# Seven PSUM areas of their own, and two instructions for a three-bank exponential

## The chip, the cores and the metric

The kernel runs on one core of a Trainium2 chip. The metric is the device time of one execution in microseconds, lower being better. A run's profile is one execution recorded by the hardware profiler; its span goes from the first to the last instruction. PE is the matrix engine (PEld its weight loads), ACT the scalar engine, DVE the vector engine, POOL a third elementwise engine, SP the queue that issues most DMAs.

## The reference

One input `x` of 2048 rows by 640 columns goes through a layer norm. Attention with 32 heads of 20 columns reads it, and so does a gated layer with 1728 hidden columns. The attention output is multiplied by a silu of the gated layer, and `x` is added:

```python
xn = _layernorm(x)
qkv = (xn @ wqkv).reshape(B, S, 3, 32, 20).transpose(2, 0, 3, 1, 4)
p = softmax(einsum("bhqd,bhkd->bhqk", q, k) * 20 ** -0.5)
s = einsum("bhqk,bhkd->bhqd", p, v).transpose(0, 2, 1, 3).reshape(B, S, D) @ wo
h = sigmoid(xn @ w_gate) * (xn @ w_up)
out = x + s * silu(h @ w_down)
```

The weights are `wqkv` 640 x 1920, `wo` 640 x 640, `w_gate` and `w_up` 640 x 1728, `w_down` 1728 x 640. Everything is bf16 at the borders.

## The kernel before

**Start.** The rows come in four chunks of 512. DVE makes the statistics, ACT and POOL write the normalised tiles `xn` (two each per chunk, lines 244 and 247), PE transposes them (line 252), ACT and DVE copy the result to `xnT` (lines 256 and 258). The keys of the first group of heads and the first queries follow.

**Attention.** Four heads make a group; there are eight groups and four chunks of 512 queries, so 32 blocks, each with 16 key tiles x 4 heads = 64 score jobs. A job is one score matmul of 32 x 128 by 32 x 512 into one PSUM bank (2 KB per partition; there are eight banks), an exponential, and one value matmul that adds 21 x 512 into a quarter of the accumulator `oacc`, one bank. Score matmuls of up to four heads run side by side on PE, and so do four value matmuls.

The exponential has two ways. On ACT (`exp_act`, line 81) one instruction takes a whole slot of PSUM: `scA3` has three banks, `scA2` two, and they alternate. On DVE it is made of integers: `iv` (line 747) reads one bank, `scD`, and after four heads of a key tile four passes `pb` (line 625) follow over all of them, and the value matmul is done for each pass (so four times, with scaled values `vs`). At most four of the 16 key tiles of a block go this way; `claim_dve` gives them out and `claim_act` the others.

**Side work.** Keys, queries and values of the next blocks, the gated layer (gate and up `mk_gu`, tanh `tnh` on ACT, product `hT` on DVE, then the down projection `mk_down` with `td` and `gqs`, which is parked in DRAM as `gq_dram`) and the output projection (`mk_out`, one piece per 128 rows and half of the columns) all use one bank, `misc`, one after another: a piece has its matmuls, then its ACT and DVE steps, and only then does the bank go to the next.

**Normalisation.** At a block's end DVE copies `oacc` to `on` (line 593). The row sums go through DRAM (`ld`, `lt`), are inverted (`rt`, line 603), go through DRAM again (`rd`, `rl`), POOL multiplies (line 610), and DMAs put the block into `oU` with heads along partitions, as the output projection needs it.

**Order.** The orders of PE, ACT and DVE are fixed while the kernel is built, by a planner that steps a clock (`now`) and has a cost for each instruction (`T_F`, `T_PV`, `T_MM`, a charge `T_MODE` where PE changes between score matmuls, F, value matmuls, PV, and side work, M). Its clock only sets the order; on the chip each engine goes through its list and waits for semaphores. Pieces of the gated layer are tied to blocks 0 to 27 and taken one at a time as `misc` comes free. What is left when the blocks end is written out behind them, piece by piece. The buffers for ACT's exponentials are `pt0` (three of three banks) and `pt1` (four of two):

```python
SLOT = (3, 2)
scA = [psum.tile([P, n, 512], FP32, name=f"scA{n}", tag=f"scA{n}") for n in SLOT]
scD = psum.tile([P, 512], FP32, name="scD", tag="scD")
NPT, NPB, NIV = (3, 4), 2, 2
```

## Time and profile before

| | us |
|---|---|
| median of 3 runs | 966.5 (958.08 to 977.37) |
| the profiled execution | 965.4 |
| its span | 963.7 |
| PE busy | 867.8 (90%) |
| ACT busy | 802.9 (83%) |
| DVE busy | 768.1 (80%) |
| POOL busy | 107.3 (11%) |

Busy time counts an instruction from its start to its end. On ACT, DVE and PE the next one can begin before that end, so the pace of an engine is read from one start to the next, in the timeline. An idle time in brackets is that of the engine before the row, with what ended it. Names such as `scA_428` carry a buffer number: 428 is the slot of three banks, 429 that of two. A view can join rows that follow each other (`x4`).

### The profile page before, as it was taken

What the parts mean: (1) busy time and instruction counts of PE and PEld (TensorE: products, weight loads), DVE (VectorE), ACT (ScalarE), POOL (GpSimd) and SP (SyncE); (2) the same over time, 40 slices, a digit from 0 to 9 for tenths busy, and PEclk for the clock granted to TensorE, in tenths of its full rate; (3) what the DMA queues carried; (4) which work ended last, traced back from release to release, by engine and by line L of the source; (5) the groups of instructions that cost most, each with busy time, mean ns of one, the idle gap of its engine ahead of it and who ended that gap; (6) DMA issues with size and microseconds to landing.
All of it is one profiled execution on the core that took longest, in us unless ns stands there. A gap on an engine that the chain in (4) does not pass through costs nothing.

```text
span 963.7 us, 18399 instructions
## 1 busy us (share of the span) xinstructions
PE 867.8 (90%) x7285; PEld 306.8 (32%) x7372; DVE 768.1 (80%) x1302; ACT 802.9 (83%) x790; POOL 107.3 (11%) x152
## 2 busy tenths in 40 slices
PE   3799999999999999999999999999999999997664
PEld 1333323333333233332333333333233322223332
DVE  6588889898888888888888889898888888883122
ACT  3769998989999898979999999999999899981000
POOL 4110010110001000100000000110000000000044
PEclk9799999999999999999999999999999999998889
DMA  8301211112110211111110111102121111211366
GB/s 215 126 10 43 49 44 33 47 48 53 30 38 29 52 44 41 45 42 46 45 42 20 41 33 44 44 16 64 44 58 30 38 50 45 62 44 31 109 185 184
DMA packets 85798, 54.53 MB, mean 57 GB/s; under 512 B 33552, under 2 KB 79440, under 8 KB 85712
## 3 DMA queue, kind: packets, MB, share of 16 engines
q1 hardware_dynamic: 84560, 52.05, 19.7%
q8 instruction: 57, 0.93, 0.4%
q10 hardware_dynamic: 1152, 1.31, 0.4%
q14 instruction: 29, 0.24, 0.1%
HBM read 42.32 MB, written 8.39 MB: 53 GB/s over the span
## 4 chain that ended last, share of the span: by engine, by line
PE 49%; ACT 24%; DVE 18%; issue 5%; DMA 3%; POOL 1%; SPq 0%; POOLq 0%; DVEq 0%; another core or an unknown queue 0%; ACTq 0%
PE oacc L580 13%; PE mps L402 10%; DVE pb L625 7%; PE scA_428 L540 6%; PE mps L425 5%; DVE iv L747 5%; PE scA_429 L540 5%; PE scD L540 4%; PE mps L457 2%; PE mps L372 2%; PE mps L341 1%; DVE ob L464 1%; PE mps L352 1%; DMA ob<-gq_dram 1%; DVE hT L410 1%
## 5 line engine op out<-in xcount | busy, mean ns | idle before, releaser
L747 DVE TENSOR_SCALAR iv<-scD 128x512 int16<-128x512 f32 x452 | 310.0, 686 | 95.4 <-PE scD L540 85.9
L625 DVE TENSOR_SCALAR pb<-iv 128x2048 int16<-128x2048 int16 x452 | 307.9, 714 | 3.0
L402 PE MATMUL mps<-xnT,wgu 128*128 128x512 bf16 (+1 forms) x505 | 150.9, 385 | 7.7 <-DVE hT L410 1.4
L610 POOL TENSOR_TENSOR on_bf<-on,rl 128x512 bf16<-128x512 f32 x32 | 42.7, 1335 | 558.0 <-DMA rl<-rd 341.6
L540 PE MATMUL scD<-q,kT_69 32*128 32x512 bf16 x228 | 87.9, 385 | 2.3 <-DVE iv L747 1.8
L425 PE MATMUL mps<-wd,hT 128*128 128x320 bf16 x448 | 80.9, 306 | 8.6 <-DVE gqs L435 7.5
L540 PE MATMUL scD<-q,kT_70 32*128 32x512 bf16 x224 | 85.6, 382 | 2.1 <-DVE iv L747 1.8
L580 PE MATMUL oacc<-pb,vs_74 128*21 128x512 bf16 x684 | 80.2, 382 | 1.7 <-DVE pb L625 1.2
L580 PE MATMUL oacc<-pb,vs_73 128*21 128x512 bf16 x672 | 79.7, 382 | 1.6 <-DVE pb L625 1.3
L540 PEld LDWEIGHTS <-kT_70 32*128 32x128 bf16 x1024 | 38.5, 91 | 123.4 <-issue 119.4
L540 PEld LDWEIGHTS <-kT_69 32*128 32x128 bf16 x1024 | 39.2, 91 | 120.8 <-issue 113.9
L402 PEld LDWEIGHTS <-wgu 128*128 128x128 bf16 (+1 forms) x560 | 44.1, 98 | 85.1 <-issue 58.4
L540 PE MATMUL scA_428<-q,kT_69 32*128 32x512 bf16 x478 | 64.5, 387 | 7.4 <-DVE q L168 3.2
L540 PE MATMUL scA_428<-q,kT_70 32*128 32x512 bf16 x480 | 64.8, 383 | 4.6 <-ACT pt_2941 L81 0.5
L540 PE MATMUL scA_429<-q,kT_70 32*128 32x512 bf16 x320 | 64.0, 383 | 1.4 <-ACT pt_3070 L81 0.4
L540 PE MATMUL scA_429<-q,kT_69 32*128 32x512 bf16 x318 | 63.3, 386 | 1.4 <-ACT pt_7252 L81 0.5
L425 PEld LDWEIGHTS <-hT 128*128 128x128 bf16 x448 | 38.9, 98 | 49.4 <-issue 37.4
L457 PE MATMUL mps<-wo,oU 128*128 128x320 bf16 x160 | 31.2, 332 | 23.1 <-DVE ob L464 22.1
L464 DVE SCALAR_TENSOR_TENSOR ob<-mps,ob 128x320 f32<-128x320 f32 x32 | 15.7, 492 | 38.2 <-PE mps L457 31.1
L81 ACT ACTIVATE tnh<-mps 128x512 bf16<-128x512 f32 (+1 forms) x56 | 35.6, 636 | 10.5 <-PE mps L402 10.5
L410 DVE SCALAR_TENSOR_TENSOR hT<-tnh,mps 128x512 bf16<-128x512 bf16 (+1 forms) x56 | 38.1, 681 | 4.4 <-PE mps L402 3.9
L580 PEld LDWEIGHTS <-v_71 128*21 128x21 bf16 x1024 | 27.7, 90 | 41.1 <-issue 33.0
(1374 smaller groups left out, 1754.5 us busy)
## 6 DMA issues: line engine op xcount, KB each, us to landing
rl<-rd SPq DMA_DIRECT2D x128, 64.0 KB
wgu<-in_B_w_gate_dram SPq DMA_DIRECT2D x24, 320.0 KB
wgu<-in_B_w_up_dram SPq DMA_DIRECT2D x24, 320.0 KB
gq_dram<-gqs SPq DMA_DIRECT2D x32, 160.0 KB
ob<-gq_dram SPq DMA_DIRECT2D x16, 320.0 KB
ob<-in_A_x_dram SPq DMA_DIRECT2D x16, 160.0 KB
out_dram<-ob SPq DMA_DIRECT2D x16, 160.0 KB
oU<-on_bf SPq DMA_DIRECT2D x112, 20.0 KB
```

Of the source, the lines that this page charges most:

```text
L81: return nc.scalar.add_instruction(mybir.InstActivation(func=func, name=nc.get_next_instruction_name(), engine=ENG.Activation, ins=[nc.sca ...
L372: nc.tensor.matmul(st["ps"][:, i * 2 * GC:(i + 1) * 2 * GC], lhsT=xnT[:, kd, tts[i] * P:(tts[i] + 1) * P], rhs=wvs[pr][:, kd, :], start=(k ...
L402: nc.tensor.matmul(st[key][0:fs, :], lhsT=w[:, i, kd, ko * P:ko * P + fs], rhs=xnT[:, kd, c * QC:(c + 1) * QC], start=(kd == 0), stop=(kd ...
L410: nc.vector.scalar_tensor_tensor(out=hT[0:fs, kf, :], in0=st["t"][0:fs, :], scalar=1.0, in1=st["u"][0:fs, :], op0=ALU.add, op1=ALU.mult)
L425: nc.tensor.matmul(st["ps"][:, 0:HD], lhsT=hT[0:fsz[kf], kf, t4 * P:(t4 + 1) * P], rhs=wd[0:fsz[kf], kf, h * HD:(h + 1) * HD], start=(kf = ...
L457: nc.tensor.matmul(st["ps"][:, 0:HD], lhsT=oU[:, kd, tt * P:(tt + 1) * P], rhs=wo[:, kd, h * HD:(h + 1) * HD], start=(kd == 0), stop=(kd = ...
L464: nc.vector.scalar_tensor_tensor(out=tmp, in0=st["ps"][:, 0:HD], scalar=0.25, in1=gqr[:, sl], op0=ALU.mult, op1=ALU.mult)
L540: nc.tensor.matmul(dst, lhsT=kTs[(b // NQC) % 2][32 * j:32 * j + 32, kt * P:(kt + 1) * P], rhs=qs[b][32 * j:32 * j + 32, :], start=True, s ...
L580: nc.tensor.matmul(oacc[32 * j:32 * j + DH + 1, :], lhsT=lhsT, rhs=u["src"], start=first, stop=last, tile_position=(0, 32 * j), skip_group ...
L610: nc.gpsimd.tensor_tensor(out=on_bf, in0=on, in1=rl, op=ALU.mult)
L625: nc.vector.tensor_scalar(out=pb[:, k, :, :].bitcast(I16), in0=iv, scalar1=0.25, scalar2=cst, op0=ALU.mult, op1=ALU.add)
L747: nc.vector.tensor_scalar(out=d["iv"][:, j, :], in0=scD, scalar1=I_OFF, scalar2=I_LOW, op0=ALU.add, op1=ALU.max)
```

## The change

The eight banks are divided anew: two slots of two banks (`scA`), three single banks (`bank`), which are tensors of their own, and `oacc`. A fill of a slot has two banks, or three where the single bank with the slot's number (0 or 1) is free. Such a fill is two ACT instructions, one over the single bank and one over the slot. Single banks are also used by the DVE way and by side work: bank 2 first, and banks 0 and 1 for side work only when it is behind a schedule (`due`), which spreads it evenly to a little before the last four blocks. The gated layer is no longer tied to blocks but taken whenever this schedule has room. Several side pieces can be under way, and their later steps wait for events (`pre`, `gates`).

The planner is rewritten with it: other costs, a step of 0.02 instead of 0.04, rules on when PE leaves one kind of matmul for another (`URGENT`, `HOLD`, `ROUNDS`), alternation of `iv` and passes (`SLACK`), and no new DVE tile in a block with fewer than 16 ACT jobs left (`D_LAST`). The exponentials' buffers are two of two banks and four of three (`NPT`); a two-bank fill takes either.

In the start, all normalised tiles are made by DVE and all `xnT` copies by ACT. At the end, the last block isn't normalised through DRAM: PE transposes `on`, DVE divides, PE transposes back, and the output projection of the last 512 rows is split into a part over the first seven groups, which needs no last block, and one matmul per piece for the last group (`tail_steps`). Its operands are loaded ahead (`tail_load`).

```diff
-                if i % 2 == 0:
-                    nc.scalar.activation(out=xn[:, i, :], in_=xt[:, i, :], func=ACT.Identity,
-                                         bias=nb[:, i, :], scale=rstd[:, i, :])
-                else:
-                    nc.gpsimd.tensor_scalar(out=xn[:, i, :], in0=xt[:, i, :], scalar1=rstd[:, i, :],
-                                            scalar2=nb[:, i, :], op0=ALU.mult, op1=ALU.add)
+                nc.vector.tensor_scalar(out=xn[:, i, :], in0=xt[:, i, :], scalar1=rstd[:, i, :],
+                                        scalar2=nb[:, i, :], op0=ALU.mult, op1=ALU.add)
...
-                if kd % 2 == 0:
-                    nc.scalar.copy(out=dst, in_=tp)
-                else:
-                    nc.vector.tensor_copy(out=dst, in_=tp)
+                nc.scalar.copy(out=dst, in_=tp)
...
-    SLOT = (3, 2)
-    scA = [psum.tile([P, n, 512], FP32, name=f"scA{n}", tag=f"scA{n}") for n in SLOT]
-    scD = psum.tile([P, 512], FP32, name="scD", tag="scD")
+    SLOT = 3
+    scA = [psum.tile([P, 2, 512], FP32, name=f"scA{i}", tag=f"scA{i}") for i in range(2)]
+    bank = [psum.tile([P, 512], FP32, name=f"bk{i}", tag=f"bk{i}") for i in range(3)]
...
-    LAT = 0.07
-    D_WAIT = 0.0
-    T_F, T_PV, T_MM, T_MODE = 0.215, 0.216, 0.216, 0.10
-    T_IV, T_PASS, T_ON = 0.655, 0.63, 0.66
-    NPT, NPB, NIV = (3, 4), 2, 2
+    EL, PL = 0.15, 0.21
+    T_F, T_PV, T_MM, T_MODE = 0.2133, 0.2133, 0.2133, 0.107
+    T_IV, T_PASS, T_ON = 0.605, 0.605, 0.60
+    NPT, NPB, NIV = (2, 4), 2, 2
...
     def claim_dve():
-        for b in range(claimed[0] // NJOB, min(NBLK, claimed[0] // NJOB + 2)):
-            if d_left[b]:
+        for b in range(base(), min(NBLK, base() + 2)):
+            if d_left[b] and len(a_left[b]) >= (D_LAST if b < NBLK - 1 else D_LAST_END):
                 if q_at.get(b, 1e9) > now:
                     return None
                 claimed[0] += GH
                 return b, d_left[b].pop(0)
...
+        def due():
+            return total * min(1.0, progress() / (NBLK - NQC - 0.2))
...
+                        w = 2 if m <= 2 and buf_free(pt_left[2], NPT[0]) else 3
+                        if buf_free(pt_left[w], NPT[w - 2]):
+                            pt = w2.tile([P, w, QC], BF16, tag=f"pt{w}", bufs=NPT[w - 2], name=f"pt{w}")
...
+                            if m == SLOT:
+                                exp_act(pt[:, 2, :], bank[nexp % 2])
+                            exp_act(pt[:, 0:min(m, 2), :], scA[nexp % 2][:, 0:min(m, 2), :])
...
+                        behind = done < due() + LAG
+                        for f in ((2, (nfill + 1) % 2, nfill % 2) if behind else (2,)):
+                            if flex[f] <= now:
+                                m_bank = f
+                                break
...
+                    want = SLOT if flex[nfill % 2] <= now and d_bank != nfill % 2 else SLOT - 1
...
+    def tail_steps():
...
+        on = w2.tile([P, QC], FP32, tag="on", bufs=2, name="on")
+        nc.vector.tensor_copy(out=on, in_=oacc)
+        early(mains[0], 0, slice(0, 512), False)
+        early(mains[1], 1, slice(0, 512), False)
+        tps = scA[0][:, 0, :]
+        for i in range(4):
+            nc.tensor.transpose(out=tps[:, i * P:(i + 1) * P], in_=on[:, i * P:(i + 1) * P], identity=ident_f)
...
+        nc.vector.reciprocal(out=rq, in_=tpv[:, :, :, 0:1])
...
+        early(mains[2], 2, slice(0, 512), False)
+        early(mains[3], 3, slice(0, 512), False)
...
+            nc.tensor.transpose(out=tp2[0:GC, i * P:(i + 1) * P], in_=onq[:, i, :], identity=ident)
...
+        for t4 in range(4):
+            late_mm(mains[t4], t4, slice(0, 512))
...
+            nc.vector.scalar_tensor_tensor(out=tmp, in0=mains[t4], scalar=0.25, in1=gqr[:, 0:512],
+                                           op0=ALU.mult, op1=ALU.mult)
+            eng = nc.gpsimd if t4 < 2 else nc.vector
+            eng.tensor_tensor(out=ot[:, 0:512], in0=tmp, in1=xr[:, 0:512], op=ALU.add)
...
```

More of the change, by code (lines that the diff above doesn't have):

```diff
@@ L204 @@
         make_identity(nc, ident)
+        nc.gpsimd.tensor_copy(out=ident_f, in_=ident)
         for w in wqks:
@@ L646 @@
         blk_loaded = -1
-        misc_at = 0.0
-        extra = []
+        active = []
         norm_pending = None
-        STEP = 0.04
+        STEP = 0.02
         def progress():
-            return claimed[0] / NJOB
+            return min(claimed[0] / NJOB, base() + 0.99)
+        total = sum(x.work for x in items + glu_items if x.need is None)
+        done = 0.0
+        def due():
+            return total * min(1.0, progress() / (NBLK - NQC - 0.2))
         def finish(item, t):
@@ L684 @@
-            evs = ([cur] if cur is not None else []) + extra
-            if free["ACT"] <= now:
-                it = next((e for e in evs if e.i < len(e.ops) and e.ops[e.i][0] == "ACT" and e.ready <= now), None)
-                s = slots[nexp % 2]
+            if not tail and not glu_items and q_at.get(NBLK - 1, 1e9) <= now and not any(
+                    it.need is None for it in items + active):
+                tail_load()
+            active = [it for it in active if it.i < len(it.ops)]
```

428 lines of the change are left out of this document (247 added, 181 removed).

## The prediction

> **What bounds the kernel now.** I read the page's totals first, then busy time by stage, with the cuts at the first score matmul and at the last copy of the output accumulator.
>
> ```profile
> PE 867.8 (90%) x7285; PEld 306.8 (32%) x7372; DVE 768.1 (80%) x1302; ACT 802.9 (83%) x790; POOL 107.3 (11%) x152
> PEclk9799999999999999999999999999999999998889
> 0.00:38.70 38.70, 15.90 (x104) 8.83 (x106) 21.78 (x72) 19.79 (x32) 14.07 (x34) 0.96 0.60 154
> 38.70:872.40 833.70, 798.14 (x6899) 268.34 (x6985) 724.44 (x1186) 778.98 (x749) 66.66 (x85) 0.99 0.16 44
> 872.40:963.70 91.30, 53.77 (x282) 29.59 (x281) 21.85 (x44) 4.09 (x9) 26.54 (x33) 0.87 0.45 134
> ```
>
> The window rows give length, then busy time of PE, PEld, DVE, ACT, POOL, granted clock, DMA share, GB/s. There are three stages: 38.7 us of start, 833.7 us of attention, and 91.3 us of tail in which ACT does 4 us of work. Their sum is the span, 963.7; the profiled run took 965.4, so 1.7 lie around it. That run is 1.1 below the median of the three timed ones, 966.5.
>
> The tail, from the timeline (start, length, what, idle time before it and what ended that):
>
> ```profile
> 893.37 2.17 PE L425 MATMUL mps<-wd,hT 128*128 128x320 bf16 x14 [1.05 <-DVE gqs L435]
> 895.57 0.44 ACT L81 ACTIVATE td<-mps 128x320 bf16<-128x320 f32 x1 [2.78 <-PE mps L425]
> 896.04 0.49 DVE L435 SCALAR_TENSOR_TENSOR gqs<-td,mps 128x320 f32<-128x320 bf16 x1 [2.72 <-ACT td L81]
> 896.58 2.17 PE L425 MATMUL mps<-wd,hT 128*128 128x320 bf16 x14 [1.05 <-DVE gqs L435]
> 949.76 0.84 PE L457 MATMUL mps<-wo,oU 128*128 128x320 bf16 x5 [0.64 <-DVE ob L464]
> 950.70 0.49 DVE L464 SCALAR_TENSOR_TENSOR ob<-mps,ob 128x320 f32<-128x320 f32 x1 [1.00 <-POOL ob L466]
> 951.25 0.84 PE L457 MATMUL mps<-wo,oU 128*128 128x320 bf16 x5 [0.65 <-DVE ob L464]
> 960.17 0.79 POOL L466 TENSOR_TENSOR ob<-ob 128x320 bf16<-128x320 f32 x1 [0.60 <-DVE ob L464]
> ```
>
> With one bank for side work, matmuls, ACT and DVE take turns: 3.2 us for each of eight down-projection pieces, then about 1.49 us for each of 32 output pieces. The tail is a latency chain, not a load.
>
> For the attention stage I need the pace of ACT and of PE, from start to start:
>
> ```profile
> 587.34 1.46 ACT L81 ACTIVATE pt_7654<-scA_428 128x1536 bf16<-128x1536 f32 x1
> 588.67 1.04 ACT L81 ACTIVATE pt_7670<-scA_429 128x1024 bf16<-128x1024 f32 x1
> 589.57 0.63 ACT L81 ACTIVATE tnh<-mps 128x512 bf16<-128x512 f32 x1
> 590.05 1.49 ACT L81 ACTIVATE pt_7688<-scA_428 128x1536 bf16<-128x1536 f32 x1
> 843.05 0.39 PE L540 MATMUL scA_428<-q,kT_70 32*128 32x512 bf16 x3
> 843.38 0.40 PE L580 MATMUL oacc<-pb,v_72 128*21 128x512 bf16 x4
> 843.60 0.39 PE L580 MATMUL oacc<-pb,vs_74 128*21 128x512 bf16 x4
> 843.92 0.39 PE L540 MATMUL scA_429<-q,kT_70 32*128 32x512 bf16 x2
> ```
>
> ACT steps are 1.33 us for three banks, 0.90 for two, 0.48 for one: 0.425 per bank plus about 0.05 per instruction. A PE round (one matmul of 512 columns, or up to four small ones side by side) takes 0.22, and 0.32 where the kind of matmul changes, so a change costs about 0.107. I take 0.215 per round; for 320 columns (2.17 - 0.31)/13 = 0.143.
>
> Counted from the program: 319 exponentials of 1536, 319 of 1024 and one of 512 columns. In the stage ACT therefore needs 319 x 1.33 + 319 x 0.90 + 0.48 = 712, plus 55 tanh and 31 abs at 0.48 and 24 tanh of 320 columns at an estimated 0.32, 49 in all: 761 of 833.7, so 73 idle. PE has 2533 rounds of 512, 608 of 320, 320 of 160 (about 0.07), 80 of 128 (about a quarter of 0.215) and 1565 changes of kind: 825, of which 10 lie in the start and 41 in the tail. So 775 in the stage, 59 idle. **ACT and PE are both over 90% committed; what is lost is waiting.** These rows name part of it:
>
> ```profile
>   PE oacc L580: 25.6, 9
> ACT pt_5422 L81 <- PE oacc L580: 5.0, 1, 5.0
> ACT aq L160 <- PE mps L352: 11.8, 6, 6.4
> DVE iv L747 <- PE scD L540: 85.9, 160, 1.4
> ```
>
> Nine exponentials waited 25.6 us, at most 5.0 at once, for value matmuls to give back a buffer (the ends of blocks); an abs of the q step stood once for 6.4 us at the head of ACT's queue. DVE's 86 us before `iv` are slack: at 452 pairs of 0.60 + 0.60 it has room.
>
> **The change part by part.** *Tail.* The order of DVE at the program's end, before (`gqs` is a down piece, `ob` an output piece, `on` the copy of the accumulator):
>
> ```order
> L747 TENSOR_SCALAR iv<-scD 128x512 x2
> L625 TENSOR_SCALAR pb<-iv 128x2048 x4
> L593 COPY on<-oacc 128x512
> L410 SCALAR_TENSOR_TENSOR hT<-tnh,mps 128x512
> L603 RECIPROCAL rt<-lt 128x16
> L410 SCALAR_TENSOR_TENSOR hT<-tnh,mps 64x512
> L435 SCALAR_TENSOR_TENSOR gqs<-td,mps 128x320 x8
> L464 SCALAR_TENSOR_TENSOR ob<-mps,ob 128x320 x32
> ```
>
> And after, the same engine and place:
>
> ```order
> L644 TENSOR_SCALAR pb<-iv 128x2048 x4
> L482 SCALAR_TENSOR_TENSOR ob<-bk_434,ob 128x320 x8
> L679 COPY on<-oacc 128x512
> L687 RECIPROCAL rq<-scA_430 128x16
> L689 TENSOR_TENSOR onq<-scA_430,rq 128x320
> L697 COPY o_11896<-tp_11891 80x512
> L708 SCALAR_TENSOR_TENSOR hT<-scA_431,xnT 128x512 x2
> L708 SCALAR_TENSOR_TENSOR hT<-bk_432,xnT 128x512
> L711 TENSOR_TENSOR xnT<-hT,xnT 128x512
> ```
>
> Eight `gqs` and 24 of 32 `ob` have left the end; the last `gqs` now stands behind the 27th of 32 copies of `on`. What follows the last value matmul: 32 output matmuls on one bank, 6.4 pieces at the row's 1.49 = 9.5; `on` 0.6; four fp32 transposes, not in the trace, between 0.055 and four rounds each, say 0.8 in all; reciprocal, product and copy on DVE 1.3; four matmuls 0.9; six handovers at about 0.2; then DVE's eight last steps at 0.6 = 4.8; and 2.7 from the last add to the end, as in the row at 960.17. Sum 22, bounds 16 and 30. **Tail 91.3 to 22.** The 32 output matmuls stand on PE ahead of the tail's own, so whatever holds them holds everything. The old normalisation by DMA of the last block falls away; it was hidden under the down pieces. Eight loads for the last chunk and most of the output pieces' loads move into the last blocks, on SP ahead of the normalisation of the blocks before the last.
>
> ```profile
> 955.44 0.43 SPq L451 DMA_DIRECT2D ob<-in_A_x_dram  x1
> ```
>
> At 0.43 an issue, eight cost SP 3.4 us; the output pieces that need that normalisation come a block later, some 26 us, which covers it. I cost it at nothing, and at 3.4 if the cover is gone.
>
> *Start.* The normalised tiles leave ACT and POOL for DVE:
>
> ```profile
> 15.61 3.48 POOL L247 TENSOR_SCALAR xn<-xt,rstd,nb 128x640 bf16<-128x640 bf16 x4
> 16.55 0.71 PE L252 MATMUL tp<-ident,xn 128*128 128x128 bf16 x5 [4.39 <-POOL xn L247]
> 38.75 0.39 PE L540 MATMUL scA_428<-q,kT_69 32*128 32x512 bf16 x3 [3.16 <-DVE q L168]
> ```
>
> The 4.4 us wait for POOL goes. DVE gains 16 tiles of 640 columns, between 0.2 each (the pace of `pb`, 2048 in 0.60) and 0.75 (of `iv`, 512 in 0.60), 3 to 12 us on an engine busy 21.8 of 38.7, and loses eight copies. I take -3, bounds +2 and -6: 36.
>
> *Attention stage, loads.* Order of ACT in mid-program, before:
>
> ```order
> L81 ACTIVATE pt_7654<-scA_428 128x1536
> L81 ACTIVATE pt_7670<-scA_429 128x1024
> L81 ACTIVATE tnh<-mps 128x512
> L81 ACTIVATE pt_7688<-scA_428 128x1536
> L81 ACTIVATE pt_7703<-scA_429 128x1024
> ```
>
> And after (a three-bank fill is a `bk` row and the `scA` row behind it):
>
> ```order
> L83 ACTIVATE pt_7111<-scA_430 128x1024
> L83 ACTIVATE pt_7135<-bk_433 128x512
> L83 ACTIVATE pt_7135<-scA_431 128x1024
> L83 ACTIVATE td<-bk_432 128x320
> L83 ACTIVATE pt_7172<-scA_430 128x1024
> ```
>
> In all 722 of 1024 and 164 of 512 columns, so only 163 fills of three banks; most are two. ACT needs 722 x 0.90 + 164 x 0.48 = 729, plus 52 with the side work that came out of the tail: 781, or 20 more. PE: 2522 rounds, 568 of 320, 112 of 128, 1494 changes, 812; less 10 and 12 at the ends, 790, or 15 more (25 from the tail, less 11 rounds and some 70 changes). DVE: 440 pairs, 14 less.
>
> *Attention stage, waits.* ACT's 73 idle: DVE tiles are no longer claimed with fewer than 16 jobs of a block left, so the passes end ahead of the block; I credit 20 of the 25.6. Side work enters ACT's queue only when its matmuls are modelled as done: 6 of the abs waits. Against it stands the turn-round of a two-bank slot:
>
> ```profile
> 364.16 1.06 ACT L81 ACTIVATE pt_4635<-scA_429 128x1024 bf16<-128x1024 f32 x1
> 365.27 0.39 PE L540 MATMUL scA_429<-q,kT_70 32*128 32x512 bf16 x2 [0.22 <-ACT pt_4635 L81]
> 865.74 0.38 PE L540 MATMUL scA_428<-q,kT_70 32*128 32x512 bf16 x1
> 866.16 0.60 ACT L81 ACTIVATE pt_11377<-scA_428 128x512 bf16<-128x512 f32 x1 [0.17 <-PE scA_428 L540]
> ```
>
> Exponential to refill 1.11, refill to exponential 0.42: 1.53 of the 1.80 that two two-bank exponentials last. PE may come 0.27 late; before, the two-bank slot had 0.7. An interrupted round plus a change is 0.1 to 0.3, so mostly covered; for 427 pairs of two-bank fills I add 6, bounds 0 and 427 x 0.1 = 43. Idle 73 - 20 - 6 + 6 = 53; **stage 781 + 53 = 834**. PE then works 95% of it, against 93.
>
> **Sum:** 36 + 834 + 22 = 892, plus 1.7: 894 us, 71.7 below the profiled run and 7.5% below the median.
>
> **Rivals.** *The waiting stays as it was*: 73 idle, stage 854, total 914. For it: PE and ACT now need nearly the same time, and each waits for the other. *The stage packs tight*: two more banks for side work and for `iv` leave ACT 25 idle, as in the fully packed rows at 587 to 590; total 866. *Each instruction pays its latency*: the rows' 1.04 holds 0.2 beyond two banks, and were 247 more exponentials to pay 0.2 instead of 0.05, that adds 37: 931. The rows say 0.05, in a long run of alternating tiles. [...]
>
> *Slower: buffers of the exponentials run out at every block end.* They held 3 x 3 + 4 x 2 = 17 banks, 7.3 us of ACT; now two of two banks and four of three, mostly filled with two: 12 banks, 5.1. The accumulator has one bank still, so PE cannot begin a block's value matmuls before the copy of the last one. Should each of 31 ends cost the 5.0 of the longest wait, that is 156 in place of my 6, total 1044; it turns slower than the noise from 3 us per end. Against it: 22 of 31 ends cost nothing before. *The tail does not close*: side work falls behind in the real run and PE, in order, waits; half the 69 us come back, total 928.
>
> **Chances.** Forecast 0.46, waiting stays 0.22, tight 0.16, latency 0.04, tail 0.05, buffers in part (under 986) 0.04, slower 0.03. Range 856 to 932: it takes in both neighbours and the middle of the latency and tail cases; outside lie a third of the tight case (0.05), half of those two (0.05) and the buffers (0.07). Within 2% of the median, 947 to 986, is about what this kernel's measurement can't tell from no change. Faster 0.92, same 0.05, slower 0.03.
>
> **What would show it.** After: no 80 us tail without ACT work, under 30 us behind the last value matmul; first score matmul at 33 to 38; two-bank exponentials stepping at 0.90 and one-bank at 0.48; ACT waits for `oacc` under 10 us. I am wrong if exponentials wait for `scA` by more than 30 us in sum, if waits on `oacc` grow, or if output pieces on PE wait for `oU`.

## The result and the profile after

The changed kernel takes 930.25 us (median of four runs, 926.63 to 932.87), the kernel before 969.26 beside it: a ratio of 0.963, 95% interval 0.953 to 0.973. The forecast was 894, the range 856 to 932. The direction and the range hold; of 72 us forecast 39 came.

The page's totals of the changed kernel and the windows of its three stages, cut at the first score matmul and at the end of the last value matmul (columns as before):

```profile
PE 852.2 (92%) x7266; PEld 294.5 (32%) x7352; DVE 751.3 (81%) x1288; ACT 828.1 (90%) x1037; POOL 103.8 (11%) x138
0.00:36.21 36.21, 17.06 (x105) 8.75 (x108) 25.75 (x80) 16.98 (x32) 8.59 (x27) 0.92 0.67 176
36.21:897.66 861.45, 820.70 (x7076) 278.47 (x7160) 714.15 (x1189) 811.14 (x1005) 87.42 (x102) 0.99 0.19 54
897.66:924.80 27.14, 14.46 (x87) 7.30 (x88) 11.44 (x19) 0.00 (x0) 7.81 (x9) 0.88 0.20 66
```

This execution took 926.6 us, 1.8 of them outside the span. Against the sum of the prediction the start is 36.2 for 36, the tail 27.1 for 22, and the **attention stage 861.5 for 834**: that is where the gain went.

The new instructions run at the pace taken for them. Timeline of ACT, starts 0.90 us apart for two banks and 0.48 for one:

```profile
587.82 0.68 ACT L83 ACTIVATE pt_7754<-bk_433 128x512 bf16<-128x512 f32 x1
588.30 1.12 ACT L83 ACTIVATE pt_7754<-scA_431 128x1024 bf16<-128x1024 f32 x1
589.21 1.13 ACT L83 ACTIVATE pt_7771<-scA_430 128x1024 bf16<-128x1024 f32 x1
```

So ACT's need is the 781 us worked out, and the rest of the stage is waiting. The view of ACT's immediate instructions in the stage lists what ended its idle times (us, times), before:

```profile
  PE oacc L580: 25.6, 9
  PE scA_428 L540: 5.0, 8
  PE scD L540: 5.0, 4
  PE mps L402: 4.8, 2
  PE scA_429 L540: 1.0, 1
```

and after (L559 is the score matmul, L599 the value matmul):

```profile
  PE bk_434 L559: 13.8, 25
  PE bk_433 L559: 12.9, 19
  PE bk_432 L559: 5.8, 14
  PE oacc L599: 4.5, 7
  PE scA_431 L559: 4.3, 11
  PE scA_430 L559: 2.8, 4
```

Waiting for the accumulator fell from 25.6 to 4.5 us, waiting for score matmuls rose from 11.0 to 39.6 in 73 times. This view counts only what is left after the end of the instruction before, and successive exponentials overlap by some 0.2 us; so from here on I count each step from start to start, less the pace of its kind (1.33, 0.90, 0.48, 0.32). By that measure ACT loses 68 us in the stage before (27 on `oacc`, 14 on scores, 19 on side work at the head of its queue, the rest small) and 74 after (**5.5 on `oacc`, 56 on scores**, 1 on side work). With 781 and the 4.4 us from the last exponential to the last value matmul that gives 859 of the 861.5.

What such a wait looks like, in the timeline without the weight loads:

```profile
331.79 1.02 ACT L83 ACTIVATE pt_4310<-scA_430 128x1024 bf16<-128x1024 f32 x1
...
332.55 0.83 PE L415 MATMUL bk_432<-xnT,wgu 128*64 128x512 bf16 x3
...
333.18 1.01 ACT L83 ACTIVATE pt_4322<-scA_431 128x1024 bf16<-128x1024 f32 x1
333.31 0.60 PE L599 MATMUL oacc<-pb,vs_74 128*21 128x512 bf16 x5
...
333.97 0.38 PE L599 MATMUL oacc<-pb,vs_74 128*21 128x512 bf16 x2
334.29 0.39 PE L559 MATMUL scA_430<-q,kT_69 32*128 32x512 bf16 x2
...
334.78 1.02 ACT L83 ACTIVATE pt_4351<-scA_430 128x1024 bf16<-128x1024 f32 x1 [0.58 <-PE bk_434 L559]
```

Slot `scA_430` was free when its exponential ended at 332.81. PE did three rounds of a gate piece and four value rounds before it came back at 334.29, 1.48 us later; ACT should have begun at 333.18 + 0.90 and began 0.70 late. Of the 56 us, 39 stand behind value rounds in this way, in 95 cases, with the slot free for 0.77 us at the median. So the late refill is not the latency of the turn-round; PE is elsewhere in its list.

Sorted by which fills follow one another (waits over 0.05 us, 58 in all), 426 pairs of two-bank fills make 29 us, 0.068 each. Another 21 us stand before 132 fills of three banks that follow one of two, 0.156 each; before, 318 such neighbours cost 0.039 each. The other 8 us stand behind fills of three banks. The repeat of after gives the same: 32, 20 and 10.

### The profile page after: what moved, and what is told of

Read it like the earlier page. It is cut to its first block, busy times and chain, and to the rows that moved or that the text cites. A ratio compares the mean times of both kernels' runs of the same rounds, so it can differ in the third digit from the quotient of the medians.

```text
span 924.8 us, 18739 instructions
## 1 busy us (share of the span) xinstructions
PE 852.2 (92%) x7266; PEld 294.5 (32%) x7352; DVE 751.3 (81%) x1288; ACT 828.1 (90%) x1037; POOL 103.8 (11%) x138
## 4 chain that ended last, share of the span: by engine, by line
PE 49%; ACT 23%; DVE 18%; issue 6%; DMA 2%; SPq 1%; POOL 0%; DVEq 0%; ACTq 0%; POOLq 0%
PE oacc L599 13%; PE scA_431 L559 7%; PE scA_430 L559 6%; DVE pb L644 6%; DVE iv L844 6%; PE bk_434 L415 4%; PE bk_432 L415 3%; PE bk_433 L415 3%; PE bk_433 L438 2%; PE bk_432 L438 1%; PE bk_434 L475 1%; PE bk_434 L438 1%; PE bk_432 L365 1%; PE bk_434 L354 1%; DVE stats L236 1%
## 5 line engine op out<-in xcount | busy, mean ns | idle before, releaser
L644 DVE TENSOR_SCALAR pb<-iv 128x2048 int16<-128x2048 int16 x440 | 304.1, 715 | 2.8
L844 DVE TENSOR_SCALAR iv<-bk_434 128x512 int16<-128x512 f32 x182 | 124.5, 684 | 39.8 <-PE bk_434 L559 39.4
L844 DVE TENSOR_SCALAR iv<-bk_433 128x512 int16<-128x512 f32 x131 | 89.4, 683 | 29.6 <-PE bk_433 L559 29.3
L844 DVE TENSOR_SCALAR iv<-bk_432 128x512 int16<-128x512 f32 x127 | 86.6, 682 | 23.1 <-PE bk_432 L559 22.8
L599 PE MATMUL oacc<-pb,vs_74 128*21 128x512 bf16 x684 | 86.8, 392 | 2.8 <-DVE pb L644 2.6
L559 PEld LDWEIGHTS <-kT_69 32*128 32x128 bf16 x1024 | 38.4, 91 | 130.0 <-issue 125.3
L559 PEld LDWEIGHTS <-kT_70 32*128 32x128 bf16 x1024 | 40.1, 91 | 124.0 <-issue 117.5
L559 PE MATMUL scA_430<-q,kT_69 32*128 32x512 bf16 x367 | 73.3, 386 | 2.9 <-DVE q L172 0.8
L559 PE MATMUL scA_431<-q,kT_70 32*128 32x512 bf16 x362 | 71.1, 385 | 4.0 <-ACT pt_10982 L83 0.7
L559 PE MATMUL scA_430<-q,kT_70 32*128 32x512 bf16 x357 | 71.0, 386 | 3.2 <-ACT pt_10810 L83 0.5
L559 PE MATMUL scA_431<-q,kT_69 32*128 32x512 bf16 x359 | 71.1, 385 | 1.8 <-ACT pt_1526 L83 0.3
L599 PE MATMUL oacc<-pb,vs_73 128*21 128x512 bf16 x636 | 70.4, 381 | 0.5 <-issue 0.3
L415 PE MATMUL bk_434<-xnT,wgu 128*128 128x512 bf16 (+1 forms) x224 | 68.4, 383 | 1.2 <-issue 0.8
L438 PEld LDWEIGHTS <-hT 128*128 128x128 bf16 x448 | 35.9, 97 | 46.8 <-issue 38.1
L415 PE MATMUL bk_432<-xnT,wgu 128*128 128x512 bf16 (+1 forms) x155 | 47.6, 383 | 2.0 <-DVE iv L844 1.0
L599 PEld LDWEIGHTS <-v_72 128*21 128x21 bf16 x1024 | 31.4, 91 | 47.5 <-issue 36.8
L559 PE MATMUL bk_433<-q,kT_70 32*128 32x512 bf16 x114 | 44.4, 389 | 0.1
L415 PE MATMUL bk_433<-xnT,wgu 128*128 128x512 bf16 (+1 forms) x142 | 42.8, 383 | 1.9 <-issue 0.8
L559 PE MATMUL bk_433<-q,kT_69 32*128 32x512 bf16 x108 | 41.6, 385 | 0.0
L559 PE MATMUL bk_432<-q,kT_69 32*128 32x512 bf16 x103 | 39.9, 388 | 0.0
```

The lines of the kernel that those rows point to most:

```text
L415: nc.tensor.matmul(st[key][0:fs, :], lhsT=w[:, i, kd, ko * P:ko * P + fs], rhs=xnT[:, kd, c * QC:(c + 1) * QC], start=(kd == 0), stop=(kd ...
L438: nc.tensor.matmul(st["ps"][:, 0:HD], lhsT=hT[0:fsz[kf], kf, t4 * P:(t4 + 1) * P], rhs=wd[0:fsz[kf], kf, h * HD:(h + 1) * HD], start=(kf = ...
L559: nc.tensor.matmul(dst, lhsT=kTs[(b // NQC) % 2][32 * j:32 * j + 32, kt * P:(kt + 1) * P], rhs=qs[b][32 * j:32 * j + 32, :], start=True, s ...
L599: nc.tensor.matmul(oacc[32 * j:32 * j + DH + 1, :], lhsT=lhsT, rhs=u["src"], start=first, stop=last, tile_position=(0, 32 * j), skip_group ...
L644: nc.vector.tensor_scalar(out=pb[:, k, :, :].bitcast(I16), in0=iv, scalar1=0.25, scalar2=cst, op0=ALU.mult, op1=ALU.add)
L844: nc.vector.tensor_scalar(out=d["iv"][:, j, :], in0=bank[bk], scalar1=I_OFF, scalar2=I_LOW, op0=ALU.add, op1=ALU.max)
```

## Experiments

Medians are of the runs taken for each kernel (one run for the one-bank and the start experiments). All waits are by the start-to-start count in one profiled execution; the expectations speak of 59.6 and 44 us for after, from a first count over a slightly wider window and with a coarser sorting, where this one has 56 and 39. The kernels named lighter or short compute less than the reference asks for; what each leaves out stands in its expectation.

| kernel | time | stage | ACT lost | on scores | on `oacc` | on side work |
|---|---|---|---|---|---|---|
| before | 969.3 | 833.6 | 68 | 14 | 27 | 19 |
| after | 930.3 | 861.5 | 74 | 56 | 5.5 | 1 |
| after, repeated | 928.8 | 863.7 | 78 | 60 | 5.6 | 1 |
| five buffers | 928.9 | 865.5 | 76 | 56 | 7 | 4 |
| three buffers | 916.8 | 850.9 | 70 | 53 | 5 | 1 |
| refill first | 946.6 | 880.8 | 93 | 25 | 23 | 35 |
| handovers as measured | 931.6 | 862.7 | 74 | 66 | 2 | 0 |
| leave at 0.25 | 931.1 | 863.3 | 76 | 53 | 9 | 6 |
| leave at 0.40 | 938.7 | 868.7 | 79 | 52 | 15 | 3 |
| PE lighter by 24 | 922.8 | 857.2 | 72 | 55 | 6 | 1 |
| ACT lighter by 23.5 | 925.4 | 860.5 | 100 | 78 | 7 | 1 |
| both | 914.8 | 848.9 | 89 | 66 | 7 | 1 |
| DVE lighter by 30 | 927.3 | 858.3 | 71 | 55 | 6 | 1 |
| all three lighter | 914.2 | 844.2 | 84 | 63 | 7 | 0 |
| short value rounds | 927.6 | 855.1 | 67 | 51 | 6 | 2 |
| side work on one bank | 1071.6 | 805.5 | 31 | 21 | 3 | 1 |

**Buffers of the exponentials.** My theory after the first trace was that the order, by its rule `if full and pv_ok: nxt = "PV"`, sends PE to value rounds whenever no buffer is free (theory A). Against it stood that PE comes back too late, whatever the buffers (B), and that PE is full (C).

```diff
-    NPT, NPB, NIV = (2, 4), 2, 2
+    NPT, NPB, NIV = (2, 5), 2, 2
...
-        rl = w2.tile([P, QC], FP32, tag="rl", bufs=2, name="rl")
+        rl = w2.tile([P, QC], FP32, tag="rl", bufs=1, name="rl")
```

> One more buffer of three banks for the exponentials (five in place of four; the row of normalising factors has one buffer in place of two to make room). Theory A (the order forces value rounds ahead of a refill whenever no buffer is free; that is where the 44 us of exponentials that waited behind value rounds come from): the waits of exponentials on score matmuls fall from 59.6 us by a quarter or more, the time to 905-920 us. Theory B (turn-round: a two-bank slot is refilled too late because PE is in the middle of a round or of a change, whatever the number of buffers): waits stay at 55-62, time 925-933. Theory C (PE is simply full): the same as B, with PE's gaps in the stage as small as now.

```diff
-    NPT, NPB, NIV = (2, 4), 2, 2
+    NPT, NPB, NIV = (2, 3), 2, 2
```

> The other way: three buffers of three banks in place of four, nothing else. Theory A: waits of exponentials on score matmuls grow by 15 us or more, and the time with them, to 945-975 us. Theories B and C: no change, 925-933.

One more changed nothing, as B and C have it. One fewer made the kernel 12 to 13 us *faster*, which none of the three has. The waits view of ACT, repeated after first, then three buffers:

```profile
ACT pt L83 <- PE bk L559: 34.5, 60, 4.5
ACT pt L83 <- PE scA L559: 8.5, 17, 1.2
```

```profile
ACT pt L83 <- PE bk L559: 28.8, 62, 3.4
ACT pt L83 <- PE scA L559: 6.8, 13, 1.0
```

Waits are a little fewer and shorter, not gone. Theory A falls as the cause of the miss. The prediction's rival of buffers that run out at block ends falls by the waits on `oacc`, 5.5 us in after.

**The rule itself, the handover times, the threshold.** Four changes of what the order is built with (the fourth is the third at 0.40), and after once more as it is:

```diff
-                if full and pv_ok:
+                if full and pv_ok and not can_f:
```

> The buffers stay as they are; only the rule that puts value rounds first when no buffer is free is made weaker: where a slot of the scores can be refilled, the refill goes first and the value rounds follow. Theory A: the exponentials' waits on scores that stand behind value rounds fall from 44 us to under 25, and the time to 905-920 us, unless the waits for a free buffer, now on ACT, take their place (exponentials waiting for value matmuls, 5.5 us in after, up to 30). Theories B and C: 923-935, since more changes of kind on PE (1530 for 1494, 4 us) eat what is won.

```diff
-    EL, PL = 0.15, 0.21
+    EL, PL = 0.21, 0.28
```

> The two handover times that the order is built with are set to what the trace of after shows: refill 0.26 us after the exponential's paced step (0.21 in place of 0.15), first matmul of a fill to its exponential 0.28 in place of 0.21 beyond the matmul's pace. Theory B says that the order thinks a two-bank slot comes round 0.13 us sooner than it does and runs late by that at each pair of fills: with the true values the order makes fewer mistakes, 910-922 us. Theory A: the order was late by its own plan, no gain, 925-935.

```diff
-URGENT, ROUNDS, HOLD, SLACK, LEAD, LAG, D_LAST, D_LAST_END = 0.15, 3, 0.15, 0.8, 40.0, 8.0, 16, 0
+URGENT, ROUNDS, HOLD, SLACK, LEAD, LAG, D_LAST, D_LAST_END = 0.25, 3, 0.15, 0.8, 40.0, 8.0, 16, 0
```

> One number of the order: PE leaves value rounds and side work for a refill when less than 0.25 us are left until ACT would run dry (0.15 in after). A value round lasts 0.213 us. Theory B (refills come up while a value round is under way and are placed too late): waits of exponentials behind value rounds fall from 39 us to 20-28; PE changes kind 28 times more (3 us). If ACT's idle time falls with it: 912-922 us. If it comes back as another wait (PE falls behind, value rounds late, buffers short), 926-934.

> The same number at 0.40 us: nearly two value rounds ahead. Theory B: waits behind value rounds under 15 us. 53 changes more on PE (6 us) and 20 three-bank fills fewer. If the lateness alone made the forecast miss: 905-918 us. If waits only move: 926-936 us.

> The changed kernel once more, unaltered, on the chip of all these runs: 925-934 us, and the waits of exponentials on scores within 3 us of the 60 us in the first trace.

With the refill first, the waits on scores do fall, to 25 us, and come back elsewhere:

```profile
ACT td L83 <- PE bk L438: 14.8, 10, 1.8
ACT tnh L83 <- PE bk L415: 14.3, 10, 1.8
ACT pt L83 <- PE oacc L599: 14.0, 34, 1.6
ACT pt L83 <- PE bk L559: 10.1, 14, 3.4
```

Steps of side work now stand at the head of ACT's queue for matmuls that PE has put off, and exponentials wait for a buffer that a put-off value round holds. It is 16 us slower. True handover times and earlier refills leave the sum of the waits where it was, and the repeat of after confirms it (928.8 us, 60 us on scores); at 0.40 those behind the accumulator grew from 5.5 to 15. In these orders a wait taken from one place was paid in another. Each change also gives another order as a whole, so one run of each can't exclude an effect of a few us.

**Whose load is it.** The order of all engines is that of after; only sizes of instructions change, so what is taken off one engine isn't given to another. What a new order, built for the smaller load, would give isn't tried.

```diff
+            n = QC // 2 if kd in (2, 3) else QC
-            nc.tensor.matmul(st[key][0:fs, :], lhsT=w[:, i, kd, ko * P:ko * P + fs],
-                             rhs=xnT[:, kd, c * QC:(c + 1) * QC], start=(kd == 0), stop=(kd == KD - 1))
+            nc.tensor.matmul(st[key][0:fs, 0:n], lhsT=w[:, i, kd, ko * P:ko * P + fs],
+                             rhs=xnT[:, kd, c * QC:c * QC + n], start=(kd == 0), stop=(kd == KD - 1))
```

> The order of every engine is that of after; only matmuls are made narrower: two of the five that make up each gate and up piece cover 256 of 512 columns (half of the columns lack two fifths of their sum). That takes 112 x 2 x 0.107 = 24 us off PE and nothing off ACT. Theory C (PE is full, and its total sets the stage): the stage falls by 18-24 us, from 861 to 837-843, the time to 905-911 us. Theory B (an exponential that follows a two-bank fill has its refill late because PE is in the middle of a value round, at about 0.1 us per such fill, and PE's total is not the bound): the waits behind value rounds stay at 35-45 us and the stage falls by less than 10 us, time 918-928 us.

```diff
...
-            act_imm(st["t"][0:fs, :], st["g"][0:fs, :], ACT.Tanh, 0.5)
+            act_imm(st["t"][0:fs, 0:8], st["g"][0:fs, 0:8], ACT.Tanh, 0.5)
```

> The order of every engine is that of after; the tanh of the gated layer is taken over 8 of 512 columns (the rest of its result is zero), which takes 56 x 0.42 = 23.5 us off ACT and nothing off PE. If PE's total sets the stage (theory C), less than 8 us of it come off the time: 920-930 us. If ACT's chain of exponentials sets it, with a wait per fill on top (theory B), 18-24 us: 904-912 us.

> Both cuts together, order as in after: two of five matmuls of each gate and up piece over 256 columns (24 us off PE; half of the columns lack two fifths of their sum) and the tanh of the gated layer over 8 columns (23.5 us off ACT; the rest of its result is zero). Alone they gave 7.5 and 5 us. Theory D (the order fills PE with value rounds and side work up to the moment at which ACT would run dry, so in each stretch both engines need about the same time, and whichever is shortened, the other one paces): together they give 18-24 us, time 906-912. If the two only add, 12 us: 916-920. If neither engine paces but the handovers do, 5 us or less beyond the better one: 917-923.

```diff
+    nc.gpsimd.memset(hT, 0.0)
...
-            nc.vector.scalar_tensor_tensor(out=hT[0:fs, kf, :], in0=st["t"][0:fs, :], scalar=1.0,
-                                           in1=st["u"][0:fs, :], op0=ALU.add, op1=ALU.mult)
+            nc.vector.scalar_tensor_tensor(out=hT[0:fs, kf, 0:8], in0=st["t"][0:fs, 0:8], scalar=1.0,
+                                           in1=st["u"][0:fs, 0:8], op0=ALU.add, op1=ALU.mult)
```

> Order as in after; the product of the gated layer on DVE covers 8 of 512 columns (the rest of its result is zero), which takes nearly 0.6 us off DVE for each of 56 pieces, some 30 us, and nothing off PE and ACT. If DVE is a pacer of its own, or its steps hold the bank that the next piece waits for: 905-915 us. If PE and ACT pace each other and DVE has room: less than 8 us, 921-931.

> The three cuts at once: two of five gate and up matmuls over 256 columns (24 us off PE), tanh (23.5 us off ACT) and product (30 us off DVE) over 8 columns; the output lacks these parts. PE and ACT together gave 914.8 us. If all of the loss is two engines that pace by turns, DVE adds nothing: 911-916. If three engines pace by turns: 898-908.

Against the mean stage of the two traces of after, 862.6: 24 us less on PE give 5, 23.5 less on ACT give 2, 30 less on DVE give 4, PE and ACT together 14, all three 18 (in the two with less DVE work, where POOL also writes zeros and is busy for 14.5 and 15.5 us of the start in place of 8.6, the first score matmul comes at 39.6 and 39.9, 2 to 3 us later, so their times hide that). When PE was shortened, the waits on scores stayed (55) and PE waited more itself (idle for 49.9 us of the stage in place of 40.8); when ACT was shortened, ACT's waits on scores rose by some 20, nearly all that it had been spared. So neither engine's load alone sets the stage: theory C falls, and B in the form in which ACT's chain sets it. A cut in both is worth more (14) than the two cuts apart (7), though not the 24 that a clean exchange would give.

The differences are small, for four traces with this very attention order (after, its repeat, tail undone, start undone) have stages from 861.2 to 865.1. Since the exponentials are the same and in the same order, they can be compared one by one. From 69 to 724 us after the stage's start in after, where the granted clock is full in all these traces, the gain on after is 4.3 us with PE lighter, 0.9 with ACT, 10.7 with both, 1.2 with DVE and 15.3 with all three; the other three with after's own order lose 1.4 to 2.0. By this too the cut in both is worth more than the two apart (5.2). That PE and ACT pace the stage by turns is the reading that fits; no run shows the turns themselves.

**Short value rounds.** Every value matmul but the first of a block and head covers half of the columns:

```diff
+            w = QC if first else QC // 2
-            nc.tensor.matmul(oacc[32 * j:32 * j + DH + 1, :], lhsT=lhsT, rhs=u["src"], start=first, stop=last,
+            nc.tensor.matmul(oacc[32 * j:32 * j + DH + 1, 0:w], lhsT=lhsT, rhs=u["src"][:, 0:w], start=first, stop=last,
```

> Order as in after; every value matmul but the first of a block and head covers 256 of 512 columns (half of the sums are incomplete), so a value round takes 0.107 us in place of 0.213 and PE has some 80 us less. Theory B (the lateness is that of a refill that comes up in the middle of a value round, or behind rounds placed ahead of it): waits of exponentials behind value rounds fall from 39 us to under 15, the stage by 25-45 us, time 885-905. Theory D with no lateness of its own: as 24 us less gave 4.3, 80 us less give some 15: time 912-918, waits behind value rounds above 30.

Waits behind value rounds fell from 39 to 15 us, as B has it, and yet the time fell by only 1 to 3 and the sum of the waits by 7 to 11. The windows say where some of it went: the whole stage, and a stretch of it alike for this kernel and for after.

```profile
37.34:892.41 855.07, 781.53 (x7076) 290.05 (x7160) 715.03 (x1189) 809.82 (x1005) 87.01 (x102) 0.95 0.19 54
100.00:500.00 400.00, 372.25 (x3358) 138.63 (x3399) 333.50 (x556) 386.02 (x482) 35.99 (x43) 1.00 0.19 51
```

```profile
100.00:500.00 400.00, 386.68 (x3299) 131.26 (x3342) 325.45 (x543) 378.48 (x472) 35.47 (x43) 1.00 0.19 51
```

Where the granted clock is 1.00, ACT is busy 386.0 of 400 us in place of 378.5, so there shorter rounds do help. Over the whole stage the clock is 0.95 in place of 0.99: it is at half for 80 us in place of 22. Waits in which the exponential came over 0.6 us after the start of its last score matmul (0.42 to 0.49 is usual) rose from 11 to 24 us, nearly all of them while the clock is at half. Exponential by exponential, this kernel is 2.9 us behind after at 69 us into the stage, gains 8.7 by 471 us at full clock, and only 1.6 more to the end, with 55 us at half clock for 14. At the pace of the middle part the whole stage would gain some 18 us, an estimate. About 11 of these are lost where the clock is at half, and even all 18 are short of the 25 to 45 us that B names. This experiment is therefore no clean proof of B.

**Side work off the two banks.**

```diff
-URGENT, ROUNDS, HOLD, SLACK, LEAD, LAG, D_LAST, D_LAST_END = 0.15, 3, 0.15, 0.8, 40.0, 8.0, 16, 0
+URGENT, ROUNDS, HOLD, SLACK, LEAD, LAG, D_LAST, D_LAST_END = 0.15, 3, 0.15, 0.8, 40.0, -400.0, 16, 0
```

> Side work is kept off banks 0 and 1, so more fills have three banks (265 of 677, for 163 of 722) and an exponential has more often three banks of cover; PE changes kind 1365 times for 1494. What is left of the side work, some 45 pieces, is written out at the end. Theory B (about 0.10 us of wait per fill behind a two-bank fill, 0.04 behind a three-bank one): the waits of exponentials on scores fall from 60 to about 50 us, the stage is shorter (835-850), the tail longer by 45 pieces of 1.5-3 us (90-120); total 990-1030 us. If lateness does not depend on the cover, the waits stay at 0.083 per fill, 56 us or more.

```profile
37.65:843.18 805.53, 726.58 (x6488) 247.97 (x6563) 671.12 (x1107) 791.76 (x1021) 67.33 (x85) 0.99 0.13 35
843.18:1069.80 226.62, 141.36 (x644) 66.83 (x649) 44.77 (x77) 21.92 (x41) 21.22 (x26) 0.87 0.29 88
```

The edit does two things, for `LAG` also stands in the rule that lets value rounds go ahead of side work: with -400 that is allowed at all times, and the expectation doesn't name it. The tail was mis-sized by far (227 us), for the left-over pieces pass one bank under a low clock (0.87). But the stage is the one that packs tight: ACT loses 31 of 805.5 us, 21 on scores. Sorted by what ACT had to do while the refill was due, a refill behind a fill of two banks costs 0.025 us on average before (313 fills), 0.083 after (529) and 0.040 here (407); behind three banks 0.009, 0.029 and 0.007. The cover alone thus isn't the cause, since the same two banks cost three times as much after as before. What differs is that two-bank fills now follow one another, with 0.90 + 0.90 us for a pair in place of 0.90 + 1.33, while PE has the side work that came out of the tail between them. Here, where much of that side work is gone, the wait halves at the same cover. Nor is it the number of two-bank fills: with this run's neighbours (229 pairs of two banks, 182 changes each way, 81 pairs of three) at after's waits for each, the sum would be 58 us, as in after, and it is 23 by the same count. What is left is the side work that is gone and the freer rule on value rounds; this run doesn't part them.

**The ends undone**, one at a time. For the tail, the last block goes through DRAM and the last eight pieces through one bank; for the start, `xn` and the copies are as before.

```diff
...
-        tail_steps()
+        norm_b(NBLK - 1, on, lt)
...
+        for it in [mk_out(4 * (NQC - 1) + t4, h, 0.0) for t4 in range(4) for h in range(2)]:
```

> Only the new end is undone: the last block is normalised through DRAM, and the output pieces of the last 512 rows go one after another through one bank as before. From the trace of after, what follows the last value matmul is 27.7 us. Here the chain of the normalisation (about 21 us from the accumulator's copy to the landing of the last piece in the block before) comes first, then eight pieces at 1.49 us and the last store: 21 + 12 + 3 = 36, after the pieces of the chunk before, of which 10 us hide under the normalisation. Time 933-945 us, 5-15 above after. If the end by transposes is worth what the prediction gave it together with the side work that left the tail, the gain of the new end itself is this difference, and the rest of the 64 us that the tail lost came from the side work that is now spread over the blocks.

```profile
924.20 0.42 PE L475 MATMUL bk<-wo,oU 128*128 128x320 bf16 x1 [15.31 <-DMA oU<-on_bf]
924.72 0.49 DVE L482 SCALAR_TENSOR_TENSOR ob<-bk,ob 128x320 f32<-128x320 f32 x1 [11.02 <-PE bk L475]
925.26 1.49 PE L475 MATMUL bk<-wo,oU 128*128 128x320 bf16 x5 [0.64 <-DVE ob L482]
```

945.0 us. The stage is the same (861.2), the tail 45.7 for 27.1, more than expected: PE stands 15.3 us for the operand, and comes back at half clock (0.65 in the mean of the tail), so five matmuls take 1.49 us for 0.84 in all eight pieces. The new end is worth 18.6 us in these two traces (14.7 between the medians); the other 45.6 of the 64 that the tail lost came from the side work that is now in the blocks.

```diff
-                nc.vector.tensor_scalar(out=xn[:, i, :], in0=xt[:, i, :], scalar1=rstd[:, i, :],
-                                        scalar2=nb[:, i, :], op0=ALU.mult, op1=ALU.add)
+                if i % 2 == 0:
+                    nc.scalar.activation(out=xn[:, i, :], in_=xt[:, i, :], func=ACT.Identity,
+                                         bias=nb[:, i, :], scale=rstd[:, i, :])
+                else:
...
```

> Only the start is undone: the normalised tiles are made by ACT and POOL again, and the copies of the transposed tiles alternate between ACT and DVE. The first score matmul moves from 36.2 back to 38-39.5 us, the time by 2-3 us: 926-936 us within the spread of after.

The first score matmul moves from 36.2 to 38.6, as expected, but 36.2 is a low one: in the other traces with the new start, unless POOL writes zeros there, it comes at 36.1 to 37.9, in the repeat of after at 37.9. So the start is worth 0.8 to 2.6 us by these traces. The time of 932.8 is one run.

**Candidates.** Both start from three buffers; one holds the output pieces back (`o_at[tm[1]] = now + 15.0`), one leaves for the refill earlier (`URGENT, ROUNDS, HOLD = 0.25, 3, 0.25`).

> Candidate: three buffers of three banks (916.8 us) and, with it, output pieces held back 6 us longer after the normalisation of their block is issued (15 us in place of 9), so that PE no longer stands for the operand oU; in the trace of after that wait was 6 us with a half clock behind it. 908-916 us if the wait is worth something here, 915-920 if it was already gone in the kernel with three buffers.

> Candidate: three buffers of three banks (916.8 us) with the refill 0.25 us ahead and PE held for a slot about to come free for 0.25 us. If lateness is what is lost: 900-912 us; if waits only move: 914-924 us.

919.7 and 925.8 us: neither beats three buffers alone, 916.8, whose ratio to before is 0.945 (0.937 to 0.954). That is the best version here, 12 to 13 us ahead of after. Its stage has 4 to 8 us less of waits and a granted clock of 1.00 in place of 0.99. Why its order waits less is open; since orders of the same layout lie between 916.8 and 946.6, I take it for a luckier order, not for a virtue of three buffers.

## Why the prediction was right or wrong

**Right.** The three stages and what each can give. The start, 36.2 for 36, with some luck, since it is 36.1 to 37.9 in the other traces: four of DVE's `xn` tiles in a row take 1.50 us, about 0.33 each from start to start (within 0.2 to 0.75), and PE's wait for POOL, 4.4 us before, is gone: in the start of after its waits are for DVE and ACT alone. ACT's need, 781: the exponentials step at 0.90 and 0.48. The trace of after has the two instructions of a fill 0.48 + 0.90 apart, about 0.05 above the one of 1.33 where the rival of latency per instruction has 0.2, so that rival falls. The credit of 20 us for the accumulator's waits (22 came). That of 6 for side work at the head of ACT's queue was right in kind and too small (18 came).

**Wrong: the attention stage, 861.5 for 834.** The step that failed is "for 427 pairs of two-bank fills I add 6, bounds 0 and 427 x 0.1 = 43". The waits of exponentials on scores rose by 42, from 14 to 56. That this is the upper bound is chance: the pairs themselves wait 29 us, 0.068 each, within the bounds and five times my 6, and the rest of the rise stands at and behind fills of three banks (0.156 where one follows a fill of two, 0.039 before), for which the sum adds nothing and gives no reason. I had chosen the low value since an interrupted round plus a change, 0.1 to 0.3, nearly fitted the 0.27 by which PE may come late. The trace shows PE late by more than one round, with several value rounds and side matmuls ahead of the refill and the slot free for 0.77 us at the median. The idle time came to 80 us for my 53: 36 more on scores, 14 less by the larger credits, some 5 more in small waits and at the end. That is near the 73 of before, so the rival *the waiting stays as it was*, with 914, came nearer, and its reason, "PE and ACT now need nearly the same time, and each waits for the other", fits the lighter kernels. But the sum stayed by two changes that nearly cancel, 40 us less and 42 more. Its 854 for the stage and my 22 for the tail, each some 5 to 8 low, make the difference to 926.6.

Of the cause this much is shown: no change of the number of buffers, of the handover times in the order, of the threshold or of the rule on full buffers took the loss away; it isn't the load of PE, of ACT or of DVE alone; cuts in PE and ACT together help more than each apart; and the waits halve where side work leaves the stage and value rounds may go ahead of what remains. The greater number of three-bank fills there doesn't explain it. Why PE is elsewhere when a slot comes free stays open between the side work and the order, and nothing shows that a better order at this layout couldn't do it.

**The tail, 27.1 for 22**, is inside its bounds of 16 to 30. Its rows:

```profile
907.05 0.49 DVE L482 SCALAR_TENSOR_TENSOR ob<-bk_434,ob 128x320 f32<-128x320 f32 x1 [1.00 <-PE bk_434 L475]
907.46 0.68 DVE L679 COPY on<-oacc 128x512 f32<-128x512 f32 x1
...
909.34 0.66 PE L684 MATMUL scA_430<-ident_f,on 128*128 128x128 f32 x4
...
915.90 1.66 DVE L711 TENSOR_TENSOR xnT<-hT,xnT 128x512 bf16<-128x512 f32 x1
...
918.20 0.69 DVE L711 TENSOR_TENSOR xnT<-hT,xnT 128x512 bf16<-128x512 f32 x1
```

The output pieces ahead of the copy took 9.8 us for 9.5. No row of before showed the four fp32 transposes, whose 0.8 us, with four rounds each as the bound, was my guess; here the four take 0.66. From the copy to DVE's last step it is 13.0 us where my items give 9.6; among DVE's eight last steps one took 1.66 us for 0.69. From there to the end it is 4.4 for 2.7. The rival *the tail does not close* did not come.

**The signs named.** The tail without ACT work is 27 us, the first score matmul at 36.2, the steps 0.90 and 0.48, the waits on `oacc` 4.5 us. But exponentials waited for `scA` and the single banks by 39.6 us, over the 30 named as the sign of being wrong, and an output piece did wait for `oU`:

```profile
862.75 0.70 PE L475 MATMUL bk_434<-wo,oU 128*128 128x320 bf16 x4 [0.20 <-DVE iv L844]
865.95 0.42 PE L475 MATMUL bk_434<-wo,oU 128*128 128x320 bf16 x1 [2.49 <-DMA oU<-on_bf]
866.30 0.61 PE L559 MATMUL scA_430<-q,kT_70 32*128 32x512 bf16 x2
...
867.01 1.02 ACT L83 ACTIVATE pt_11439<-scA_430 128x1024 bf16<-128x1024 f32 x1 [3.75 <-PE bk_433 L559]
```

That cover, "a block later, some 26 us", failed once, at 3.8 us of ACT, near the 3.4 that the prediction names for it.

## What to carry to other kernels

Where two engines each need over 90% of a stage and feed each other through a few small buffers, as here, don't count on a wait to vanish when its named cause is removed: here the idle time stayed about what it was, 73 us before and 80 after. Credit a removed wait only where the engine behind it has time to spare, and size the new waits for every kind of neighbour, not only for the new one. Work that is moved out of a latency-bound tail into such a stage is not free even where it fits by the sums: 64 us left the tail here and the stage grew by 28. To learn whose load sets a stage, shorten one engine's instructions in an unchanged order, then the other's, then both.

## What the hardware showed that was not expected

**The granted clock fell without a pause of PE before it.** Around the wait for `oU`, windows of one microsecond (columns as above):

```profile
863.00:864.00 1.00, 0.45 (x4) 0.10 (x1) 0.90 (x2) 0.26 (x1) 0.00 (x0) 0.75 0.18 50
864.00:865.00 1.00, 0.00 (x0) 0.00 (x0) 0.00 (x0) 0.00 (x0) 0.00 (x0) 0.50 0.08 21
...
869.00:870.00 1.00, 1.00 (x6) 0.23 (x5) 0.06 (x1) 0.63 (x2) 0.00 (x0) 0.50 0.00 0
870.00:871.00 1.00, 1.00 (x6) 0.36 (x4) 1.00 (x2) 0.93 (x1) 0.00 (x0) 0.84 0.00 0
```

The clock is halved from about 863.5 to 870.3, and score matmuls last 0.61 us for 0.39. The pause of PE is 2.5 us, and the clock fell at its beginning, after 3.4 us in which PE was busy for 59%. So a stretch that is not idle was enough in this trace.

In all 20 traces here the clock is full or half and changes in steps of 3.41 us. Of the steps at full clock, all 55 in which PE was busy for under 49% were followed by one at half clock. So were 34 of 128 with 49 to 64%, and 5 of 4924 with more, three of these in the kernel with short value rounds. The clock doesn't explain why 24 us less on PE gave so little, for the stage's clock is 0.99 there as in after; with short value rounds, at 0.95, it is a part of it.

**Beside a POOL step, 34 of 36 passes of DVE ended behind it; the steps `iv` took no longer there.** Under the normalisation's product on POOL, a step `iv` and then a pass `pb`:

```profile
805.77 1.64 POOL L629 TENSOR_TENSOR on_bf<-on,rl 128x512 bf16<-128x512 f32 x1 [23.78 <-DMA rl<-rd]
806.20 0.68 DVE L844 TENSOR_SCALAR iv<-bk_432 128x512 int16<-128x512 f32 x1
806.92 1.05 DVE L644 TENSOR_SCALAR pb<-iv 128x2048 int16<-128x2048 int16 x1
```

The pass ends 0.55 us after POOL's step. Of the 36 passes in this trace that start under a POOL step, 34 end just so and take 0.72 to 1.76 us; in the other two POOL ends within 0.1 us of their start, and they take 0.68, as passes alone do. The 34 steps `iv` that start under a POOL step take 0.62 to 0.69 us, as they do alone. The sum of 1.66 us in the tail also ends 0.54 us after POOL's sums, while the product before it, beside the same sums, takes 0.68. My tail had eight equal steps of 0.6 and no such cost.
